# Cluster assignment by pair, later maxima, bulk digits and a new plan in a fused attention and mixture-of-experts kernel

## The chip, the cores and the metric

The kernel runs on one core of one Trainium2 chip, as one launch. The metric is the device time of one execution in microseconds. Five engines work side by side: TensorE (PE in the profile, its weight loads PEld), VectorE (DVE), ScalarE (ACT), GpSimd (POOL) and SyncE (SP), which here issues nearly all transfers. Each engine takes its instructions in the order in which the program lists them for it, and waits in front of the first one that is not ready.

## The reference

Inputs: q, k and v of 4 batches, 8 heads, 768 positions and width 64; 16 centroids a head; a gate matrix 512x8; for 8 experts w1 (512x1024) and w2 (1024x512).

```
q_assign = argmax(normalised q . normalised centroid), k_assign likewise
scores   = q k^T / 8, replaced by -1e9 where q_assign != k_assign
x        = softmax(scores) v, written as 3072 tokens x 512
expert   = argmax(x @ w_gate), gate = its softmax weight
each expert keeps its 80 tokens of largest gate
out[token] = gate * (relu(x[token] @ w1[e]) @ w2[e]), 0 for all other tokens
```

## The kernel before, in words

**Attention.** The 32 heads go in 16 pairs, four to a batch. Both heads of a pair lie in one 128-partition tile of k (`ldk`) and of q (`ldq`). For each head an operand KAB and an operand QAB are put together in SBUF: the high and the low part of the values (a cast on ScalarE, a subtraction on GpSimd, `pair`, L245), and 16 rows with the one-hot code of the cluster, all of it copied into place by small transfers on SP's queue (`copy`, L71). A query whose cluster has no key is masked there.

The cluster codes come from `assign` (L188): a matmul with the normalised centroids, a transpose, a maximum and an equality on VectorE, a transpose back, a matmul that settles ties, and an evacuation on ScalarE. It runs once a batch for k and once for q, over all four pairs, in two halves of 384 columns.

A pair is 12 units, a unit being one head and one chunk of 128 keys. In a unit, TensorE computes scores twice. `sm` (L432) has queries on the partitions, and VectorE takes each row's maximum from it (`mx`, L434). Six such maxima of a head are gathered in `mr`, transposed on TensorE (L452), evacuated on ScalarE (`row`, L455), and a 3 KB transfer on SP's queue writes them as one more row into QAB. After that `st` (L469, then L470, which holds this row) has keys on the partitions, ScalarE takes the exponential (`pp`, L475), GpSimd adds the six chunks of a head (`sum`, L484), and TensorE multiplies with the values (`av`, L493). So the first `st` of a head cannot start before its row has landed. Finished heads are transposed, scaled, and written out as tokens `xs`, with logits and gates for each batch.

**Maxima for scaling.** While attention runs, the 32 blocks of w1 are loaded once, one after the other, into a single buffer (`weigh`, L1333), and VectorE takes each one's largest magnitude (`most`, L1335). `most` is also taken from every pair's values (`ldv`, L1324). These maxima set the scales of the half-precision operands of the experts. Each of these reductions stands in VectorE's one queue, among the `mx`.

**Selection and experts.** `digits` (L627) cuts every gate's bits into five digits and compares them with all digit values; `select` (L684) finds each expert's 80th largest gate digit by digit, a count on TensorE for each digit. Then tokens are gathered and the experts run: `hp` (L1013) and `yp` (L1041). The second matrix of an expert is either split in a high and a low part (three matmuls of two halves each, 48 instructions) or taken as plain fp32 (named in `native2`; 16 instructions that run longer).

**What sets the order.** The kernel builds its instruction lists itself. Work is cut into steps (an engine, an assumed cost, what it needs, a due time `at`) in lanes; `Flow.run` picks, step by step, the engine that could start first, and on it the step that is due first. So the numbers in `CFG`, the assumed costs and the due times set the order on every engine, and nothing is decided at run time. Where TensorE would stand idle by the plan, `fill` (L1511) puts in small matmuls whose results are not used (L1418, here called fillers).

## Time and profile before

| | us |
|---|---|
| three runs | 641.37, 635.55, 641.95; median 641.37 |
| the profiled execution | 639.99 |
| its span, first to last instruction | 638.0 |
| TensorE busy in the span | 590.8 |
| VectorE | 430.8 |
| GpSimd | 405.2 |
| ScalarE | 333.0 |

The profile is of one execution, whose span is 2 us shorter than its own time. Matmuls are pipelined, so groups of matmuls overlap, and a group's mean is longer than the distance from one to the next. The clock column is the mean granted clock of TensorE as a part of 2.4 GHz; 0.50 is 1.2 GHz. A stretch's length less its busy time on TensorE times the clock is the time that TensorE lost in it, by waiting or by the lower clock.

### The profile page before, as it was taken

Reading aid. Unit: us, or ns where it says so; the run is one execution under the profiler, and the core shown is the slowest. Engines: PE = TensorE matmul, PEld = TensorE weight load, DVE = VectorE, ACT = ScalarE, POOL = GpSimd, SP = SyncE. Lnnn points to the kernel's source line nnn. Section 1 sums busy time; section 2 is a strip of 40 time slices with the busy share of each in tenths; the row PEclk is TensorE's granted clock in tenths of the full one; section 3 lists DMA queues with packets and bytes.
Section 4 is the critical chain, followed back from the end, with each engine's and each line's share of the span. In section 5 each row is a group of like instructions: output and inputs, shape, how many; then the busy total and the mean of one; then the engine's idle time right before and its main releaser. Section 6 shows DMA issues by size and latency. Waiting matters only on the chain.

```text
span 638.0 us, 12227 instructions
## 1 busy us (share of the span) xinstructions
PE 590.8 (93%) x4516; PEld 402.2 (63%) x4516; DVE 430.8 (68%) x798; ACT 333.0 (52%) x706; POOL 405.2 (64%) x231
## 2 busy tenths in 40 slices
PE   8979999899969899997799988999999798999996
PEld 6666566566646666655466665666666488777664
DVE  4945677676557665764577766777779467789983
ACT  6543456565535556553355754565556270358850
POOL 5355486879567658966566778598698420454472
PEclk9998999999979899998799998999999979999999
DMA  8477755779967456999485489747593184699911
GB/s 274 100 222 169 196 160 155 173 200 280 221 191 184 142 156 157 237 314 198 125 206 142 114 216 232 207 106 190 155 340 129 28 338 160 240 363 325 397 36 32
DMA packets 71995, 124.55 MB, mean 195 GB/s; under 512 B 10848, under 2 KB 36096, under 8 KB 71936
## 3 DMA queue, kind: packets, MB, share of 16 engines
q1 hardware_dynamic: 70912, 121.12, 66.6%
q0 software_dynamic: 1024, 2.64, 1.3%
q8 instruction: 36, 0.59, 0.4%
q14 instruction: 23, 0.19, 0.1%
HBM read 70.97 MB, written 13.99 MB: 133 GB/s over the span
## 4 chain that ended last, share of the span: by engine, by line
PE 59%; DMA 19%; issue 10%; DVE 5%; SPq 3%; ACT 2%; POOL 2%; POOLq 0%; ACTq 0%; DVEq 0%
PE av L493 18%; PE sm L432 11%; PE st L469 10%; PE st L470 9%; DMA out_dram<-room,si 7%; DMA weigh<-in_w_dram 4%; SPq L72 3%; DMA xg<-xs,gi 2%; DMA QAB<-ohq 2%; PE misc L531 2%; PE misc L203 2%; PE misc L514 1%; DVE mx L434 1%; POOL xg L952 1%; DMA ldv<-in_v_dram 1%
## 5 line engine op out<-in xcount | busy, mean ns | idle before, releaser
L434 DVE TENSOR_REDUCE mx<-sm 128x1 f32<-128x384 f32 x384 | 202.5, 552 | 99.3 <-PE sm L432 96.7
L484 POOL TENSOR_TENSOR sum<-sum,pp 128x768 f32<-128x768 f32 x128 | 231.9, 1833 | 56.9 <-ACT pp L475 56.4
L475 ACT ACTIVATE pp<-st 128x384 f32<-128x384 f32 x384 | 177.5, 493 | 131.4 <-PE st L470 118.3
L432 PE MATMUL sm<-KAB,QAB 80*128 80x384 f32 x384 | 139.2, 387 | 21.7 <-DVE mx L434 8.5
L493 PE MATMUL av<-pp,ldv 128*64 128x384 f32 x768 | 142.9, 505 | 0.0
L469 PE MATMUL st<-QAB,KAB 128*128 128x384 f32 x384 | 138.9, 362 | 0.1
L470 PE MATMUL st<-QAB,KAB 81*128 81x384 f32 x384 | 134.9, 351 | 1.3 <-DMA QAB<-row 1.3
L432 PEld LDWEIGHTS sm<-KAB,QAB 80*128 80x128 f32 x384 | 72.1, 197 | 64.2 <-issue 22.9
L484 POOL TENSOR_TENSOR sum<-pp 128x768 f32<-128x768 f32 x32 | 58.6, 1847 | 59.7 <-ACT pp L475 54.4
L493 PEld LDWEIGHTS av<-pp,ldv 128*64 128x64 f32 x768 | 49.9, 139 | 62.1 <-issue 58.8
L469 PEld LDWEIGHTS st<-QAB,KAB 128*128 128x128 f32 x384 | 76.3, 199 | 7.4 <-issue 5.2
L470 PEld LDWEIGHTS st<-QAB,KAB 81*128 81x128 f32 x384 | 76.6, 199 | 1.6 <-DMA QAB<-row 1.6
L1335 DVE TENSOR_REDUCE most<-weigh 128x1 f32<-128x1024 f32 x32 | 38.9, 1215 | 29.1 <-DMA weigh<-in_w_dram 29.1
L1418 PEld LDWEIGHTS <-one 128*128 128x128 f16 x742 | 44.6, 101 | 5.6 <-issue 2.8
L952 POOL DMA_INDIRECT xg<-xs,gi x8 | 20.0, 2503 | 43.9 <-issue 26.8
L1071 POOL DMA_INDIRECT out_dram<-room,si x8 | 26.0, 3254 | 29.1 <-DVE room L1066 20.5
L298 POOL TENSOR_TENSOR ldq<-ldq,hi 128x768 fp32r<-128x768 f32 x15 | 27.4, 1829 | 16.5 <-ACT hi L292 16.4
L268 POOL TENSOR_TENSOR ldk<-ldk,hi 128x768 fp32r<-128x768 f32 x15 | 27.3, 1822 | 6.4 <-DVE mx L434 6.4
L1013 PEld LDWEIGHTS <-w1p 128*128 128x128 f16 x768 | 28.4, 100 | 3.1 <-issue 3.1
L1418 PE MATMUL tot<-K,one 128*128 128x128 f16 x447 | 29.8, 227 | 0.0
L1013 PE MATMUL hp<-xt,w1p 128*128 128x80 f16 x768 | 28.8, 202 | 0.0
L929 DVE SCALAR_TENSOR_TENSOR w1p<-raw,scales,w1p 128x1024 f16<-128x1024 f32 x22 | 27.8, 1275 | 0.0
(246 smaller groups left out, 663.2 us busy)
## 6 DMA issues: line engine op xcount, KB each, us to landing
raw<-in_w_dram SPq DMA_DIRECT2D x38, 512.0 KB
weigh<-in_w_dram SPq DMA_DIRECT2D x32, 512.0 KB
KAB<-hi SPq DMA_DIRECT2D x60, 192.0 KB
QAB<-hi SPq DMA_DIRECT2D x30, 384.0 KB
room<-in_w_dram SPq DMA_DIRECT2D x22, 512.0 KB
ldk<-in_kT_dram SPq DMA_DIRECT2D x16, 384.0 KB
ldq<-in_qT_dram SPq DMA_DIRECT2D x16, 384.0 KB
ldv<-in_v_dram SPq DMA_DIRECT2D x16, 384.0 KB
```

The source lines that it names most:

```text
L298: nc.gpsimd.tensor_tensor(lo, t, hi.bitcast(F32), op=ALU.subtract)
L432: nc.tensor.matmul(s, lhsT=qj, rhs=k[0:D + C, 0, f * HS:(f + 1) * HS], start=True, stop=True)
L434: nc.vector.tensor_reduce(mx[:, j, f:f + 1], s, axis=AX.X, op=ALU.max)
L469: nc.tensor.matmul(s, lhsT=k[:, 1, ks], rhs=q[:, 1, qs], start=True, stop=False)
L470: nc.tensor.matmul(s, lhsT=k[0:D + C + 1, 0, ks], rhs=q[0:D + C + 1, 0, qs], start=False, stop=True)
L475: self.nc.scalar.activation(self.st["pp", g, c][:, f], self.st.pop(("s", g, c, f)), AF.Exp, scale=float(self.D) ** -0.5)
L484: eng.tensor_tensor(flat(t), flat(a), flat(self.st["pp", g, c]), op=ALU.add)
L493: nc.tensor.matmul(a[i * D:(i + 1) * D, f, 0:HS], lhsT=v[:, c, i, :], rhs=st["pp", 2 * r + i, c][:, f], start=(c == 0), stop=(c == NC - 1) ...
L929: nc.vector.scalar_tensor_tensor(t[:, 1], raw, s, t[:, 0], op0=ALU.mult, op1=ALU.subtract)
L1013: nc.tensor.matmul(hp[:, f, :], lhsT=wt[:, a, fs], rhs=xt[:, x, k, :], start=(k == 0 and i == 0), stop=(k == K - 1 and i == 2))
L1335: nc.vector.tensor_reduce(self.most[:, R + n:R + n + 1], t, axis=AX.X, op=ALU.max, apply_absolute_value=True)
L1418: nc.tensor.matmul(out, lhsT=self.one16, rhs=self.K16[:, 0:n], start=True, stop=True, skip_group_check=True)
```

## The change

- Assignment: `assign` takes one pair, with the two halves of k and the two of q in the four quarters of the partitions. It is listed with the start of pair r for pair r+2, before `pair`. Codes are copied in 16x384 pieces, 8 transfers a pair in place of 4. One matmul with one column and two small VectorE operations are added to each chain.
- Loads: k and q have three buffers each in place of five. The load of pair r+3 waits for pair r's last use of its buffers; before, all eight loads of a batch were listed at the start of the batch ahead of it. `pps` gives nine exponential buffers in place of seven.
- Maxima: the due time of a `weigh` maximum moves from unit u+3 to u+6 and its load is taken to end 6 later than it was; a `ldv` maximum moves by four units and waits for an `av` of the pair before. The weigh loads start at unit 8 and are 4.5 units apart (16 and 5.1 before).
- The last six additions of exponentials run on VectorE (before all 160 on GpSimd).
- `digits` computes all five digits in six operations a call. It is called twice: for the first 18 columns and for the last batch's 6.
- Six experts, not four, take w2 as plain fp32.
- A filler's assumed cost is one value. There are 272 fillers in all, 742 before: 53, 69 and 150 in the tiles misc, st and tot, 190, 105 and 447 before.
- All due times and several assumed costs have new values.

The diff, cut to its core:

```diff
-CFG = dict(at=dict(sum=-3.18, av=5.0, xT=4.47, lt=0.61, turn=5.75, sm=3.25, exp=-0.88, mx=-0.86), stick=1.93, wait=0.03,
-           idle=0.25, dummy=128, bias=1.2, side=(9.63, 3.62, 26.8, 0.78), prep=(-0.91, 0.1), lead=(-39.88, -34.2, -42.52, -44.97,
-           -19.27), zero=(-15.03, 0.1, -6.09, -0.08, -10.39, 0.67), start=dict(pe=6.1, act=4.8, dve=7.5, pool=2.5, dma=0.0),
-           warm=48, nab=6, pps=7, sums=8, xts=4, vs=2, skew=4, raws=4, weigh=(16, 5.1), slots=(15, 9), native1=(), native2=(0, 2,
-           4, 6), early=((2, 6), 185.8), scaled=(), spread=(), mix=dict(ld=-24.41, st=-20.84, hi1=-8.36, lo1=-10.24, hi2=-13.6,
-           lo2=3.85, xg=-31.7, xp=-16.32, out=11.04, sc=-11.17, a0=4, a1=2, a2=3, spare=0.15))
+CFG = dict(at=dict(sum=0.05, av=6.35, xT=17.0, lt=4.45, turn=9.29, sm=1.01, exp=-3.24, mx=-0.7), stick=1.88, wait=0.06, idle=0.25,
+           dummy=128, bias=0.52, side=(-1.86, 0.07), prep=(0.22, 0.32), lead=(-39.03, -34.88, -36.45, -49.02, -17.95),
+           zero=(-12.17, 0.04, -13.76, 0.26), start=dict(pe=6.1, act=4.8, dve=7.5, pool=2.5, dma=0.0), warm=48, nab=6, pps=9,
+           sums=8, xts=4, vs=2, skew=4, raws=4, lds=3, keys=1, adds=6, weigh=(8, 4.5, 6.0), slots=(16, 8), native1=(), native2=(0,
+           1, 2, 3, 4, 5), early=((2, 6), 185.8), scaled=(), spread=(), mix=dict(ld=-27.65, st=-20.84, hi1=-8.36, lo1=-6.37,
+           hi2=-5.09, lo2=3.68, xg=-34.07, xp=-7.98, out=8.16, sc=-9.03, a0=6, a1=2, a2=5, spare=0.15))
-            t = self.ld.tile([P, self.S], F32, name="ld" + n, bufs=self.NP + 1)
+            t = self.ld.tile([P, self.S], F32, name="ld" + n, bufs=CFG["lds"])
-    def assign(self, b, n):
-
-        nc, S, C, NC, NP, HS, w, st = self.nc, self.S, self.C, self.NC, self.NP, self.HS, self.work, self.st
-        G = 2 * NP
-        R = G * C
-        NJ = HS // P
-
-        aside = b == 0 and n == "q"
-        lock = "spare" if aside else "misc"
 ...
+    def assign(self, b, p):
+
+        nc, C, HS, w, st = self.nc, self.C, self.HS, self.work, self.st
+        k, q = st["k", b, p], st["q", b, p]
+        NJ, G = HS // P, P // C
+        r = b * self.NP + p
+        fs = [slice(f * HS, (f + 1) * HS) for f in range(2)]
+        yield Step("pe", .71, needs=["cdiag", ("ld", "k", b, p), ("ld", "q", b, p)], take="misc", key=("sim", b, p), kind=2, seq=True)
+        sim = self.misc([P, HS])
+        for i, (t, f) in enumerate(((k, 0), (k, 1), (q, 0), (q, 1))):
+            nc.tensor.matmul(sim[32 * i:32 * i + 32, :], lhsT=self.cdiag[:, p, :], rhs=t[:, fs[f]],
+                             start=True, stop=True, tile_position=(0, 32 * i))
+        yield Step("act", .5, give="misc")
 ...
+        yield Step("act", .58, also=("dve", .75), needs=[("hi", "q", *divmod(r - 2, self.NP))] if r > 2 else [])
+        oh = st["oh", b, p] = w.tile([P, HS], F32R, name="oh", bufs=2)
+        nc.scalar.activation(oh[0:64], fi[0:64, 0:HS], AF.Identity, bias=self.negone[0:64])
+        z = w.tile([P, 1], F32, name="z", bufs=2)
+        z16 = w.tile([P, 1], F16, name="zh", bufs=2)
+        nc.vector.tensor_reduce(z[0:64], fi[0:64, 0:HS], axis=AX.X, op=ALU.max)
+        nc.vector.tensor_scalar(z16[0:64], z[0:64], 0.5, None, op0=ALU.is_gt)
+        yield Step("pe", .1)
+        nc.tensor.matmul(fi[:, HS:HS + 1], lhsT=self.twos[0:64], rhs=z16[0:64], start=True, stop=True)
+        yield Step("dve", .15)
+        ne = w.tile([P, 1], F32, name="ne", bufs=2)
+        nc.vector.tensor_scalar(ne, fi[:, HS:HS + 1], 0.5, BIG, op0=ALU.is_gt, op1=ALU.mult)
+        yield Step("act", .58, give="misc", key=("oh", b, p))
+        nc.scalar.activation(oh[64:P], fi[64:P, 0:HS], AF.Relu, scale=ne[64:P])
-                r = (2 * p + i) * C
-                copy(AB[g][D:D + C, 0, :], self.st["oh" + n, b][r:r + C, :])
-            if p == self.NP - 1:
-                flow.end["onehot", n, b] = flow.end["hi", n, b, p]
+                for f in range(2):
+                    r = 64 * (n == "q") + 32 * f + i * C
+                    copy(AB[g][D:D + C, 0, f * HS:(f + 1) * HS], self.st["oh", b, p][r:r + C, :])
-        yield Step("none", 0.0, needs=[("oh", "k", b)], key=("hi", "k", b, p), dma=[.14] * 2)
+        yield Step("none", 0.0, needs=[("oh", b, p)], key=("hi", "k", b, p), dma=[.1] * 4)
-            nc.tensor.matmul(mask, lhsT=self.sel[:, p, :], rhs=self.st["ohq", b][:, fs], start=True, stop=True)
-            yield Step("dve", .5, give="misc")
 ...
-        for l, (sh, d0, ge, pre) in enumerate(self.levels):
-            nk = ge.shape[2]
-            di, pi = T("di"), T("pi")
-            key = [("ge", l), ("pre", l)] if t0 else [None, None]
-            yield Step("dve", .5 if t0 else .95, key=key[0], port=BOTH)
-            nc.vector.tensor_scalar(di, bits, sh, 31 if l else 63, op0=ALU.logical_shift_right, op1=ALU.bitwise_and)
-            at = self.view["iota"][:, d0 + 1:d0 + nk + 1]
-            nc.vector.tensor_tensor(ge[:, t0:t1], di.unsqueeze(2).broadcast_to([P, n, nk]),
-                                    at.unsqueeze(1).broadcast_to([P, n, nk]), op=ALU.is_ge)
-            if sh:
-                yield Step("dve", .36 if t0 else .5, key=key[1], port=BOTH)
-                nc.vector.tensor_scalar(pi, bits, sh, (1 << (26 - sh)) - 1, op0=ALU.logical_shift_right, op1=ALU.bitwise_and)
-                nc.vector.tensor_tensor(pre[:, t0:t1], self.OH[:, t0:t1], pi.unsqueeze(2).broadcast_to([P, n, E]), op=ALU.mult)
+        yield Step("dve", 1.2 if long else .8, key=None if long else ("ge", 0), port=BOTH)
+        nc.vector.tensor_scalar(m, self.G[:, js].bitcast(I32), (1 << 26) - 1, None, op0=ALU.bitwise_and)
+        nc.vector.tensor_tensor(pi, m.unsqueeze(1).broadcast_to([P, L, n]), self.sh.unsqueeze(2).broadcast_to([P, L, n]), op=ALU.logical_shift_right)
+        nc.vector.tensor_tensor(self.ge0[:, js], pi[:, 0].unsqueeze(2).broadcast_to([P, n, n0]), iota(self.lowest, n0).unsqueeze(1).broadcast_to([P, n, n0]), op=ALU.is_ge)
+        yield Step("dve", .95 if long else .4, key=None if long else ("pre", 0), port=BOTH)
+        nc.vector.tensor_tensor(self.part[:, :, js], self.OH[:, js].unsqueeze(1).broadcast_to([P, L - 1, n, E]),
+                                pi[:, 0:L - 1].unsqueeze(3).broadcast_to([P, L - 1, n, E]), op=ALU.mult)
+        yield Step("dve", 2.6 if long else 1.1, key=None if long else ("ge", 1), port=BOTH)
+        nc.vector.tensor_scalar(di, pi[:, 1:], 31, None, op0=ALU.bitwise_and)
+        nc.vector.tensor_tensor(self.ge[:, :, js], di.unsqueeze(3).broadcast_to([P, L - 1, n, 31]),
-        for p in range(NP):
+        for p in range(CFG["lds"]):
-            if b + 1 < B and (p, k) == (0, 0):
-                flow.add(*(Lane(loads(b + 1, n)) for n in "kq"))
-                A = CFG["side"]
-                later(side, (self.assign(b + 1, "k"), A[0], A[3]), (self.assign(b + 1, "q"), A[1], A[3]))
             if k == 0 and r + 2 < R:
                 b2, p2 = divmod(r + 2, NP)
+                later(side, (self.assign(b2, p2), *CFG["side"]))
-                yield Step("dve", .88, key=("span", r), needs=[("ldv", r)], at=NU * r - 2)
+                yield Step("dve", .88, key=("span", r), needs=[("ldv", r)] + [("av", r - 1, 3 // K * K + K - 1)] * (r > 0), at=NU * r + 2)
-                yield Step("dma", 1.46, key=("wl", n), needs=[("st", units[u][0] * NC + units[u][1], 0)] + [("wm", n - 1)] * (n > 0), at=u)
+                yield Step("dma", 1.46, key=("wl", n), late=CFG["weigh"][2], needs=[("st", units[u][0] * NC + units[u][1], 0)] + [("wm", n - 1)] * (n > 0), at=u)
-                yield Step("dve", 1.15, key=("wm", n), needs=[("wl", n)], at=u + 3)
+                yield Step("dve", 1.15, key=("wm", n), needs=[("wl", n)], at=u + 6)
-                yield Step("pool", 1.82, alt=("dve", .92) if t >= N - 3 else None, port=BOTH, key=("sum", g, c), needs=[("exp", t, 1), ("exp", when[g, 0], 1)] + room, at=t + at["sum"])
+                yield Step(*(("dve", .95) if t >= N - CFG["adds"] else ("pool", 1.82)), port=BOTH, key=("sum", g, c), needs=[("exp", t, 1), ("exp", when[g, 0], 1)] + room, at=t + at["sum"])
-            d = CFG["dummy"] / 2350 * (1 if self.work.get(tick - 1, 0.0) >= 3060 else 2)
+            d = CFG["dummy"] / 1175
```

How it moves instructions, at three places.

TensorE between the transpose of a second head's maxima (L452, now L448) and the first `st` that needs the row. First the kernel before, fifth pair; the row goes into QAB_101, whose first `st` stands three rows below the last one shown:

```order
L452 MATMUL misc<-K,mr 6x128
L493 MATMUL av<-pp,ldv 64x384 x8
L432 MATMUL sm<-KAB_108,QAB_102 128x384 x2
L469 MATMUL st<-QAB_99,KAB_105 128x384
L470 MATMUL st<-QAB_99,KAB_105 128x384
L469 MATMUL st<-QAB_99,KAB_105 128x384
L470 MATMUL st<-QAB_99,KAB_105 128x384
L469 MATMUL st<-QAB_100,KAB_106 128x384
L470 MATMUL st<-QAB_100,KAB_106 128x384
L493 MATMUL av<-pp,ldv 64x384 x4
L432 MATMUL sm<-KAB_108,QAB_102 128x384 x2
L469 MATMUL st<-QAB_100,KAB_106 128x384
```

Then the change, fourth pair; the row goes into QAB_105, and the last row shown is the first that reads it:

```order
L448 MATMUL misc<-K,mr 6x128
L210 MATMUL misc<-K,ss 128x128 x3
L428 MATMUL sm<-KAB_112,QAB_106 128x384 x2
L465 MATMUL st<-QAB_104,KAB_110 128x384
L466 MATMUL st<-QAB_104,KAB_110 128x384
L489 MATMUL av<-pp,ldv 64x384 x4
L510 MATMUL misc<-K,xT 128x128 x3
L428 MATMUL sm<-KAB_112,QAB_106 128x384 x2
L465 MATMUL st<-QAB_105,KAB_111 128x384
L466 MATMUL st<-QAB_105,KAB_111 128x384
```

Before, two sets of `av` and four `sm` with seven `st` stood in between; now one set of four `av`, four `sm`, two `st` and six small transposes.

VectorE around the eighth `weigh` maximum. Of the `mx` in the kernel before, the last five ahead of the maximum are listed after its load, which is issued on SP:

```order
L444 TENSOR_REDUCE mr<-mx 128x6
L434 TENSOR_REDUCE mx<-sm 128x1 x4
L561 TENSOR_SCALAR den<-misc 128x24
L562 RECIPROCAL rec<-den 128x24
L565 TENSOR_TENSOR l<-misc,rec 128x3x8x8
L434 TENSOR_REDUCE mx<-sm 128x1 x2
L561 TENSOR_SCALAR den<-misc 128x24
L562 RECIPROCAL rec<-den 128x24
L565 TENSOR_TENSOR l<-misc,rec 128x3x8x8
L434 TENSOR_REDUCE mx<-sm 128x1
L1335 TENSOR_REDUCE most<-weigh 128x1
```

In the change, nine are:

```order
L1322 TENSOR_REDUCE most<-weigh 128x1
L430 TENSOR_REDUCE mx<-sm 128x1 x3
L232 TENSOR_REDUCE z<-misc 64x1
L233 TENSOR_SCALAR zh<-z 64x1
L430 TENSOR_REDUCE mx<-sm 128x1 x2
L238 TENSOR_SCALAR ne<-misc 128x1
L430 TENSOR_REDUCE mx<-sm 128x1 x3
L440 TENSOR_REDUCE mr<-mx 128x6
L284 SCALAR_TENSOR_TENSOR ldq<-misc,ldq 128x384
L430 TENSOR_REDUCE mx<-sm 128x1 x2
L1322 TENSOR_REDUCE most<-weigh 128x1
```

Over all 32 maxima there were between 1 and 8 such `mx`, median 5; now there are between 6 and 13, median 9, for all but the last two, which have none but other work.

VectorE at the end of attention, before (`most` is followed by the step that makes the scales, and by digits of the first 18 columns):

```order
L1324 TENSOR_REDUCE most<-ldv 128x1
L434 TENSOR_REDUCE mx<-sm 128x1 x7
L444 TENSOR_REDUCE mr<-mx 128x6
L1335 TENSOR_REDUCE most<-weigh 128x1
L1339 TENSOR_REDUCE m<-most 128x1
L1340 TENSOR_REDUCE m<-most 128x8
L650 TENSOR_SCALAR di<-G 128x18
L652 TENSOR_TENSOR dug<-di,K 128x450
L656 TENSOR_SCALAR pi<-G 128x18
L657 TENSOR_TENSOR dug<-OH,pi 128x144
L1345 COPY m<-misc 128x9
L1347 TENSOR_SCALAR mt<-m 128x9
```

and in the change:

```order
L1311 TENSOR_REDUCE most<-ldv 128x1
L644 TENSOR_TENSOR dug<-OH,pi 128x4x144
L647 TENSOR_SCALAR di<-pi 128x4x18
L648 TENSOR_TENSOR dug<-di,K 128x4x558
L1322 TENSOR_REDUCE most<-weigh 128x1
L480 TENSOR_TENSOR sum<-sum,pp 128x768 x6
L1322 TENSOR_REDUCE most<-weigh 128x1
L1326 TENSOR_REDUCE m<-most 128x1
L1327 TENSOR_REDUCE m<-most 128x8
L1332 COPY m<-misc 128x9
L1334 TENSOR_SCALAR mt<-m 128x9
L1335 TENSOR_SCALAR mt<-mt 128x9
```

The bulk digits of the first 18 columns stand ahead of the six additions, and the last maximum and the scales behind them.

## Rows read from the trace of the kernel before

**Rows 1.** The page's first lines: span, and busy time of each engine.

```profile
span 638.0 us, 12227 instructions
...
PE 590.8 (93%) x4516; PEld 402.2 (63%) x4516; DVE 430.8 (68%) x798; ACT 333.0 (52%) x706; POOL 405.2 (64%) x231
```

**Rows 2.** Stretches by stage: from and to, length, busy time of PE, PEld, DVE, ACT and POOL with the number of instructions, granted clock, DMA share, GB/s. They are the attention, its last sums and logits, the selection and gathers, the experts.

```profile
45.00:498.00 453.00, 424.19 (x2384) 277.87 (x2386) 300.98 (x565) 240.53 (x563) 331.17 (x185) 0.95 0.71 188
498.00:511.00 13.00, 9.03 (x112) 4.92 (x108) 4.33 (x13) 2.51 (x6) 4.03 (x2) 0.98 0.14 34
511.00:548.00 37.00, 33.62 (x542) 31.72 (x542) 24.63 (x77) 12.75 (x16) 6.53 (x11) 0.91 0.68 247
548.00:633.00 85.00, 83.83 (x1057) 57.01 (x1057) 69.95 (x76) 50.28 (x66) 42.33 (x13) 1.00 0.69 245
```

**Rows 3.** The same columns for shorter stretches of the attention.

```profile
40.00:55.00 15.00, 11.03 (x88) 8.97 (x87) 3.25 (x6) 4.17 (x10) 10.33 (x7) 0.77 1.00 247
72.00:82.00 10.00, 8.40 (x38) 6.28 (x37) 5.39 (x12) 5.53 (x14) 3.00 (x2) 0.83 0.75 204
120.00:130.00 10.00, 7.78 (x35) 4.28 (x34) 4.00 (x8) 2.97 (x7) 5.94 (x4) 0.83 0.87 220
174.00:190.00 16.00, 10.81 (x54) 6.86 (x53) 9.10 (x22) 4.98 (x12) 11.50 (x7) 0.79 0.67 193
212.00:225.00 13.00, 11.21 (x51) 8.13 (x53) 6.83 (x13) 6.44 (x15) 9.20 (x6) 0.74 0.40 121
...
286.00:300.00 14.00, 10.66 (x68) 7.41 (x65) 6.19 (x14) 4.46 (x10) 8.85 (x6) 0.88 1.04 207
300.00:316.00 16.00, 12.75 (x61) 8.62 (x59) 8.37 (x21) 6.88 (x18) 9.70 (x6) 0.79 0.51 137
...
390.00:400.00 10.00, 8.19 (x37) 4.51 (x36) 4.68 (x10) 2.93 (x7) 6.23 (x4) 0.83 0.84 206
```

**Rows 4.** The same columns for a late stretch of the attention.

```profile
450.00:495.00 45.00, 44.94 (x251) 28.88 (x249) 36.68 (x53) 25.43 (x62) 36.02 (x21) 1.00 0.59 201
```

**Rows 5.** Who waited for whom: us in total, times, longest.

```profile
DVE most L1335 <- DMA weigh<-in_w_dram: 29.1, 16, 5.5
...
DVE most L1324 <- DMA ldv<-in_v_dram: 11.9, 6, 6.5
```

**Rows 6.** The chain of waits, in order of time: start, length, what. Two loads whose maximum stood in the chain.

```profile
174.10 6.61 DMA weigh<-in_w_dram
...
286.12 6.98 DMA ldv<-in_v_dram
```

**Rows 7.** The chain of waits around the row of the fourth head: its transpose, the transfer of the row, and the `st` that reads it.

```profile
71.16 0.11 PE misc L452
...
73.33 3.27 DMA QAB<-row
...
76.65 0.44 PE st L470
```

**Rows 8.** SP's queue in order of time, just ahead of that transfer.

```profile
70.38 2.87 SPq L72 DMA_DIRECT2D KAB<-hi  x4
```

**Rows 9.** TensorE in order of time at the start of the attention: fillers, and the first `sm` behind them.

```profile
40.76 3.12 PE L1418 MATMUL misc<-K,one 128*128 128x128 f16 x53
...
47.84 0.98 PE L432 MATMUL sm<-KAB,QAB 80*128 80x384 f32 x2 [3.97 <-DMA QAB<-ldq]
```

**Rows 10.** TensorE in order of time around the selection: fillers of the first and the second digit, and the count that follows the first.

```profile
513.75 4.23 PE L1418 MATMUL tot<-K,one 128*128 128x128 f16 x42
517.91 0.76 PE L703 MATMUL q<-dug,alive 128*8 128x31 f16 x24
...
520.84 1.40 PE L1418 MATMUL tot<-K,one 128*128 128x128 f16 x22
```

**Rows 11.** VectorE in order of time: a digit of the first 18 columns while GpSimd adds, and a digit of the last batch.

```profile
488.58 2.30 DVE L652 TENSOR_TENSOR dug<-di,K 128x558 f16<-128x558 int32 x1
...
514.19 1.69 DVE L650 TENSOR_SCALAR di<-G 128x6 int32<-128x6 int32 x1
515.91 0.35 DVE L652 TENSOR_TENSOR dug<-di,K 128x186 f16<-128x186 int32 x1
```

**Rows 12.** GpSimd in order of time: its last two additions.

```profile
497.94 4.09 POOL L484 TENSOR_TENSOR sum<-sum,pp 128x768 f32<-128x768 f32 x2
```

**Rows 13.** Groups by line: busy us, mean ns of one, idle time before them.

```profile
L434 DVE TENSOR_REDUCE mx<-sm 128x1 f32<-128x384 f32 x384 | 202.5, 552 | 99.3 <-PE sm L432 96.7
...
L1335 DVE TENSOR_REDUCE most<-weigh 128x1 f32<-128x1024 f32 x32 | 38.9, 1215 | 29.1 <-DMA weigh<-in_w_dram 29.1
...
L945 DVE TENSOR_TENSOR w2p<-raw,w2p 128x1024 fp32r<-128x1024 f32 x8 | 9.4, 1214 | 0.0
```

**Rows 14.** TensorE in order of time in the experts: fillers, one expert's output from plain fp32, and the first and the last `yp` of one with split weights.

```profile
553.78 7.07 PE L1041 MATMUL yp<-room,hh 128*80 128x512 f32 x16
560.98 1.17 PE L1418 MATMUL tot<-K,one 128*128 128x128 f16 x18
...
565.96 0.45 PE L1041 MATMUL yp<-w2p,hh 128*80 128x512 f32 x1
...
571.31 0.39 PE L1041 MATMUL yp<-w2p,hh 128*80 128x512 f32 x1
...
609.96 1.11 PE L1418 MATMUL tot<-K,one 128*128 128x128 f16 x17
```

More of the change, by code (lines that the diff above doesn't have):

```diff
@@ L1428, in stream @@
             flow.add(lane)
[L1429 removed]
+        for lane, g, o, d in zip((side, prep), (self.assign(0, 1), self.pair(0, 1)), Z[::2], Z[1::2]):
             lane.add(g, at=(o, d))
[L1431 to L1433 removed]
+        flow.add(side, prep, last, tail, *(Lane(g()) for g in (scores, exps, adds, spans, weighs, values, ends, maxima, tops, shifts, vs)), *(Lane(loads(n)) for n in "kq"))
         flow.run()
```

163 lines of the change are left out of this document (70 added, 93 removed).

## The prediction

> **What bounds the kernel now.** I read the page first, then the stretches, then the waits and the chain, and last the timelines of the places found. TensorE is busy for 590.8 of 638.0 us, VectorE for 430.8 [rows 1]: TensorE is the bound, and what can be won is where it stands or runs slow. The stretches say where [rows 2]: the attention from 45 to 498 us holds 424.19 us of TensorE at a clock of 0.95, so it lost 453 - 424.19 x 0.95 = 50 us; the experts at the end lose about 1 us of 85. In a good stretch the attention loses nothing: 251 matmul records in 45.0 us at full clock [rows 4], 0.18 us a record. So the 50 us are local, and the shorter stretches [rows 3] show them by the same sum: 6.5 us at 40 to 55, 3.0 at 72 to 82, 3.5 at 120 to 130, 7.5 at 174 to 190, 4.7 at 212 to 225, 4.6 at 286 to 300, 5.9 at 300 to 316, 3.2 at 390 to 400. The rest is scattered.
>
> The four of 174 to 316, 22.7 us together, have one cause. VectorE waited 29.1 us for blocks of w1 and 11.9 us for values [rows 5]. A load that stood in the chain took 6.6 to 7.0 us [rows 6], and the maximum that needs it stands in VectorE's one queue ahead of the `mx`; TensorE's `sm` waits for `mx`, and when it stands its clock falls too (0.74 to 0.88 there [rows 3]).
>
> **The change part by part**, in us against the profiled execution of 640.0 (2 over its span); the median of the runs is 641.4, and 1% of that, 6.4 us, is about what a measurement of this kernel can tell from no change.
>
> *Maxima placed later, B: -20.* Per maximum 5 `mx` stood between a load and its use, now 9. At 0.552 us each [rows 13] that is 2.8 us of VectorE's work against 5.0, and since an `mx` comes at TensorE's pace (10 or so a 5-unit block, one in about 1.2 us: 453 us for 384), it is about 6 us of time against 11. A load needs up to 7.0 [rows 6]: before it was just short, now it is met with 4 us to spare. What hides it is the queue of `mx`; where it is gone, at the end, two maxima stand behind the additions and cost 1.2 us each [rows 13]. Ends: -22.7 (all four stretches clean) and -8 (loads that queue behind more transfers take 11 us or more). I take -20, near the clean end, since 4 us of slack is more than half a load.
>
> *Start, A: -6.* At 40.76 TensorE ran fillers for 3.12 us and then waited 3.97 us for the last copy into QAB [rows 9]; the stretch lost 6.5 us beside the fillers [rows 3]. The change takes two half chains of assignment and two loads from in front of this, yet its pair 1 transfers still stand around the first row on SP's queue, and eleven more `sm` (2.0 us at 0.18) stand ahead of the first `st`. Ends -9.6 and +2; I take two thirds of the gain.
>
> *Second heads' rows, D: +9.* This is a cost. The row of a pair's second head was transposed with 12 `av`, 4 `sm` and 7 `st` ahead of the `st` that reads it; an `av` of the program is two records, so 35 records, 6.3 us. Now, for about half the pairs, 4 `av`, 4 `sm` and 3 `st` and six short transposes, 15 records and 6 of about 0.1: 3.3 us. The trace shows what a row needs: transposed at 71.16, its transfer issued at 73.33, landed 3.27 us later, read at 76.65 [rows 7], 5.5 us in all. Of these 2.1 went by behind four other transfers on SP's queue [rows 8]; without them 0.4 + 3.27, some 3.7 to 4.2. Missing per head: 0.4 to 0.9, 15 times 0.6 = 9. Ends: 0, and 15 x 3.0 = 45, the loss of 72 to 82 [rows 3] at every pair. I take 9, since in the new order few transfers stand directly ahead of the rows. The Trainium skill, "DMA: Bandwidth & Descriptors", section on the anatomy of one DMA, gives each transfer a fixed part of about 2.0 us, whatever its size. By that an estimate of the path is 2.4 us, the rows would be hidden and this term nothing; the trace, with 3.27 us for 3 KB, speaks against it.
>
> *More small pieces in the assignment, E: +2.* Fifteen one-column matmuls and 30 small VectorE operations, under 0.3 us each, beside other work; 60 more transfers on SP's queue, where four took 2.87 us to issue [rows 8], so 43 us of SP in 450 us. It delays what stands behind on that queue, rows and copies. Ends 0 and +8 (a late row of 0.6 us in every second pair, and as much for copies).
>
> *Last additions on VectorE, F: -2.* GpSimd's last two ended at 502.03 [rows 12] and the sums on TensorE waited for them. A two-operand VectorE pass over 1024 columns takes 1.214 us [rows 13], so 768 about 0.91, half of GpSimd's 2.05; six are 5.5 us, begun as the exponentials come. Behind them stand a maximum of 1.2 us [rows 13] and the small steps of the scales, ahead of the logits' evacuations on VectorE. Ends -4 and +1.
>
> *Selection, G: -6.* After the first digit, 42 fillers run from 513.75 to 517.98 while the digit they cover was done at 516.26 [rows 10, 11]: 1.7 us too many. Later digits have 22 fillers of 1.40 us behind a step, against 0.35 us of VectorE with its predecessor [rows 10, 11], 0.4 too many each. Bulk digits also take some 0.9 us of VectorE out of each of the last levels, and the first level no longer has the 1.69 us operation that stood while GpSimd worked [rows 11]: 1.7 + 3 x 0.4 + 3 x 0.9 is 5.6. The 18-column operations ran 2.30 us [rows 11] under GpSimd's additions; they now stand ahead of the additions, off TensorE's path. Ends -9 and 0.
>
> *Experts, H: +0.5.* A plain output took 7.07 us, a split one 571.70 - 565.96 = 5.74 [rows 14]; two more plain ones cost 2.7, as TensorE is the bound there (83.83 of 85.00 [rows 2]). Fillers cost 0.065 us each there (1.17 us for 18, 1.11 for 17 [rows 14]); four blocks with 65 of them, 4.3 us, become 18 in all, about 1.1: -3.2. With fewer fillers the clock can start lower; at 1.2 GHz for the first few matmuls 0 to +4, I take 1. The casts spared on ScalarE and VectorE lie beside TensorE's work.
>
> *Other stalls of the attention, C: 0.* The 9.7 us at 72, 120 and 390 and the scattered rest come from the same work in another order. Ends -8 and +5. The third loads' buffers and nine exponential buffers: nothing, a load has a pair's time, some 28 us, against 7.
>
> Sum: -20 - 6 + 9 + 2 - 2 - 6 + 0.5 = -22.5, so **618 us**.
>
> **The rivals.**
> 1. *Rows late everywhere, slower than before.* The one mechanism: the `st` of the second head waits behind SP's queue as at 72 to 82, 3.0 us at 15 pairs: +45 in place of +9, 654 us. It decides from (22.5 + 9 + 6.4) / 15 = 2.5 us a row. For it: the distance is 3.3 us and the one row that was that close did stall. Against: at that place four copies stood ahead of it [rows 8]. Chance 0.08.
> 2. *The stalls change place.* Sixty more transfers make loads later, maxima again stand in `mx`'s way: B -8, A -3, G -2, C and the others as they are: 638 us. For it: the DMA share was 0.71 over the attention [rows 2] and 1.00 or more where it stalled [rows 3]; against: there were whole batches of loads at once there, now single ones. Chance 0.20. That the change does not do what it says I exclude for the order (it is in the lists), not for the time.
> 3. *Everything is met.* Rows land in time (D 0), and a third of C goes (-5): 604 us. For it: most stretches of attention lose nothing [rows 4]. Chance 0.19.
> 4. *The clock.* Where TensorE stood its clock was 0.74 to 0.88 of full [rows 3], and in the selection, where fillers ran nearly all the time, 0.91 [rows 2]. Without 297 of the 447 fillers in tot the counts of five digits (0.76 us each at the first [rows 10]) and the start of the experts run at 1.2 GHz: G about -1, H +4, 626 us. The Trainium skill, "TensorE: Matmul & The Clock Gate", part 1, says the low clock is the default and activity lifts it; by that this rival is the rule, the rows above agree, and only how much of the work there is on the path is open. Chance 0.13.
>
> My forecast itself has 0.40. The predicted time is 618; the range 600 to 643 takes in rivals 2, 3 and 4 and leaves out the first and the far ends. Faster by over 1%: 0.40 + 0.19 + 0.13 and a quarter of rival 2, 0.77; within 1%: the rest of rival 2, 0.15; slower: 0.08.
>
> **What would show it.** B: the wait of `most` for `weigh` and `ldv`, 41 us now, under 8, and no stretch of the attention below 0.9 of clock around such a maximum. D: `st` L466 in the chain or in the waits with "QAB<-row", about 0.6 us each time; if they are absent, rival 3. A: less than 4 us lost from 35 to 55 us. G: from the last logits to the last digit 6 us less, with few fillers; a clock of 0.5 there is rival 4. H: experts about as long as 85 us. I am wrong if attention still loses 40 us, or if VectorE's wait for loads stays over 25 us.

## The result, and the profile after

The change takes 614.45 us (median of 4 runs, 612.2 to 615.43) against 638.96 us before (635.55 to 641.95): a ratio of 0.961, with a 95% interval of 0.955 to 0.968. In a later comparison it was 617.4 against 636.57 us, 0.973 (0.969 to 0.978). So a difference of 3 us between kernels of different comparisons says nothing here, and the runs of one kernel in one comparison are 3 to 16 us apart.

The prediction was 618 (600 to 643), and the profiled span moved by -25.0 where -22.5 was forecast. The total came out near, but by luck: errors in the stages cancel, as the table below shows. The page after, for [rows 1]:

```profile
span 613.0 us, 11364 instructions
...
PE 569.8 (93%) x4030; PEld 372.6 (61%) x4030; DVE 421.0 (69%) x824; ACT 317.8 (52%) x694; POOL 395.3 (64%) x225
```

I divided both traces at the same events on TensorE: the first `av`, the last sums and logits, the first count over the last batch's digits, the last digit's closing matmuls, the first expert's `hp`. Before:

```profile
53.36 1.51 PE L493 MATMUL av<-pp,ldv 128*64 128x384 f32 x8
...
501.46 2.79 PE L531 MATMUL sm<-sum,unit 128*32 128x384 f32 x32
...
511.92 0.31 PE L703 MATMUL q<-dug,OH 128*8 128x25 f16 x6 [2.50 <-DVE dug L652]
...
533.45 0.38 PE L696 MATMUL nb<-K,nf 8*128 8x8 f32 x2
...
550.35 3.60 PE L1013 MATMUL hp<-xt,w1p 128*128 128x80 f16 x96
```

After:

```profile
51.20 1.51 PE L489 MATMUL av<-pp,ldv 128*64 128x384 f32 x8
...
475.55 2.79 PE L527 MATMUL sm<-sum,unit 128*32 128x384 f32 x32
...
486.35 0.31 PE L695 MATMUL q<-dug,OH 128*8 128x25 f16 x6 [2.73 <-DVE dug L642]
...
503.63 0.59 PE L688 MATMUL nb<-K,nf 8*128 8x8 f32 x2 [0.74 <-DVE j L729]
...
522.85 5.24 PE L1005 MATMUL hp<-xt,w1p 128*128 128x80 f16 x96
```

| stretch | before | after | difference | forecast |
|---|---|---|---|---|
| start to the first `av` | 53.4 | 51.2 | -2.2 | A -6 |
| first `av` to the last sums | 448.1 | 424.4 | -23.8 | B, C, D, E, F: -11 |
| sums to the first count | 10.5 | 10.8 | +0.3 | |
| first count to the last digit | 21.5 | 17.3 | -4.3 | G -6 |
| last digit to the first expert | 16.9 | 19.2 | +2.3 | 0 |
| first expert to the end of the span | 87.7 | 90.2 | +2.5 | H +0.5 |

The attention gave twice what I had summed up, and all behind it gave nothing (+0.9) where I had 5.5. The first row is not quite like for like: 36 `sm` stand ahead of the first `av` now, 30 before, so about 1.1 us of work (six at 0.18 us) moved from the second row into the first.

Counted by pairs (48 `st` each), most of the attention's gain sits in the first pairs of the batches 1 to 3, the pairs around whose start most loads for the next batch were issued in a row before: they took 33.3, 35.0 and 38.2 us from their first `st` to the next pair's, and take 25.0, 30.2 and 29.5 now. That is 21.8 of the 27.3 us between the first `st` and the last sums. Three of the four stretches with waits for maxima lie in or next to them as well [rows 3], so this alone does not tell the two causes apart.

The stretches after, for [rows 2, 4] (columns as there): the attention, the selection with the gathers, the experts.

```profile
51.00:475.00 424.00, 407.26 (x2372) 261.59 (x2372) 291.54 (x578) 247.39 (x575) 319.32 (x178) 1.00 0.72 198
...
485.00:527.00 42.00, 31.11 (x380) 27.31 (x381) 27.89 (x73) 10.26 (x14) 12.94 (x12) 0.63 0.64 230
527.00:610.00 83.00, 80.45 (x912) 48.68 (x908) 62.94 (x71) 30.50 (x45) 39.47 (x14) 1.00 0.68 244
```

The attention now loses 424 - 407 = 17 us at a mean clock of 1.00, where it lost 50 [rows 2]. VectorE's waits for loads [rows 5] are gone: the group of the w1 maxima has no idle time ahead of it. What TensorE waits for there is the row of a second head. From the page, and from the waits of who for whom:

```profile
L1322 DVE TENSOR_REDUCE most<-weigh 128x1 f32<-128x1024 f32 x32 | 38.6, 1207 | 0.0
```

```profile
PE st L466 <- DMA QAB<-row: 9.5, 9, 2.0
...
PE misc L235 <- DVE zh L233: 2.6, 7, 0.8
```

The chain shows such a row, for [rows 7]: transposed at 64.42, transferred from 64.94, right behind the issue of one load on SP's queue, read at 68.86. Below it stands the row with the longest wait.

```profile
64.42 0.22 PE misc L448
...
64.94 3.87 DMA QAB<-row
...
68.86 0.44 PE L466 MATMUL st<-QAB,KAB 81*128 81x384 f32 x1 [0.34 <-DMA QAB<-row]
...
288.53 4.10 DMA QAB<-row
...
292.68 0.44 PE L466 MATMUL st<-QAB,KAB 81*128 81x384 f32 x1 [2.01 <-DMA QAB<-row]
```

From the transpose to the read this is 4.4 us, against a distance of 3.3 us by my count. At this row TensorE stood for 0.34 us; the nine waits range from 0.22 to 2.01 us, about 1 us each in the mean. The transfers that ended them took 3.87 to 4.65 us.

### The profile page after: what moved, and what is told of

Its sections match the earlier page's. It is cut to its first block, busy times and chain, and to the rows that moved or that the text cites. A ratio compares the mean times of both kernels' runs of the same rounds, so it can differ in the third digit from the quotient of the medians.

```text
span 613.0 us, 11364 instructions
## 1 busy us (share of the span) xinstructions
PE 569.8 (93%) x4030; PEld 372.6 (61%) x4030; DVE 421.0 (69%) x824; ACT 317.8 (52%) x694; POOL 395.3 (64%) x225
## 4 chain that ended last, share of the span: by engine, by line
PE 65%; DMA 17%; issue 9%; POOL 3%; DVE 3%; ACT 2%; SPq 1%; POOLq 0%; ACTq 0%; DVEq 0%
PE av L489 19%; PE sm L428 11%; PE st L466 11%; PE st L465 10%; DMA out_dram<-room,si 7%; DMA QAB<-row 6%; DMA xg<-xs,gi 3%; PE misc L527 2%; PE misc L510 2%; PE misc L202 2%; POOL xg L944 1%; PE misc L282 1%; POOL sum L480 1%; PE misc L448 1%; ACT row L451 1%
## 5 line engine op out<-in xcount | busy, mean ns | idle before, releaser
L471 ACT ACTIVATE pp<-st 128x384 f32<-128x384 f32 x384 | 174.4, 491 | 103.4 <-PE st L466 94.5
L480 POOL TENSOR_TENSOR sum<-sum,pp 128x768 f32<-128x768 f32 x122 | 220.0, 1833 | 5.3 <-ACT pp L471 4.5
L466 PE MATMUL st<-QAB,KAB 81*128 81x384 f32 x384 | 131.7, 343 | 9.5 <-DMA QAB<-row 9.5
L465 PE MATMUL st<-QAB,KAB 128*128 128x384 f32 x384 | 134.0, 349 | 0.0
L466 PEld LDWEIGHTS st<-QAB,KAB 81*128 81x128 f32 x384 | 73.8, 192 | 12.5 <-DMA QAB<-row 12.5
L465 PEld LDWEIGHTS st<-QAB,KAB 128*128 128x128 f32 x384 | 73.6, 192 | 6.7 <-ACT pp L471 3.2
L944 POOL DMA_INDIRECT xg<-xs,gi x8 | 24.8, 3095 | 34.0 <-issue 18.4
L1063 POOL DMA_INDIRECT out_dram<-room,si x8 | 23.9, 2985 | 33.3 <-DVE room L1058 30.1
L1322 DVE TENSOR_REDUCE most<-weigh 128x1 f32<-128x1024 f32 x32 | 38.6, 1207 | 0.0
L1014 ACT ACTIVATE hh<-hp 128x320 f32<-128x320 f32 (+1 forms) x16 | 7.0, 438 | 43.0 <-PE hp L1005 43.0
L1406 PEld LDWEIGHTS <-one 128*128 128x128 f16 x272 | 20.5, 117 | 8.0 <-issue 5.1
L514 ACT COPY x<-misc 128x384 f32<-128x384 f32 x32 | 15.4, 481 | 17.5 <-PE misc L510 17.5
```

Source lines behind the costliest of these rows:

```text
L465: nc.tensor.matmul(s, lhsT=k[:, 1, ks], rhs=q[:, 1, qs], start=True, stop=False)
L466: nc.tensor.matmul(s, lhsT=k[0:D + C + 1, 0, ks], rhs=q[0:D + C + 1, 0, qs], start=False, stop=True)
L471: self.nc.scalar.activation(self.st["pp", g, c][:, f], self.st.pop(("s", g, c, f)), AF.Exp, scale=float(self.D) ** -0.5)
L480: eng.tensor_tensor(flat(t), flat(a), flat(self.st["pp", g, c]), op=ALU.add)
L944: nc.gpsimd.indirect_dma_start(out=xg[0:Mb], out_offset=None, in_=self.xs[:, :], in_offset=bass.IndirectOffsetOnAxis(ap=gi[0:Mb, e:e + 1], ...
L1322: nc.vector.tensor_reduce(self.most[:, R + n:R + n + 1], t, axis=AX.X, op=ALU.max, apply_absolute_value=True)
```

## The experiments

Theory: the gain is that of the maxima (B), less the late rows (D); small items at the end. Rivals: the quieter loads or the new order as a whole made the gain; the clock or the fillers set the end. Each kernel was compared with the one before on its own chip: fill_more, row_slack, max_at_load and plain_four on one, max_alone, load_burst, digits_single and sums_gpsimd on a second, change_again, row_slack_25, exp_seven and no_fillers on a third. The planner makes the list anew for each, so an edit can move other instructions too; TensorE's order without the fillers is that of the change in no_fillers, up to the experts in digits_single, and up to the last sums in sums_gpsimd. The assignment by pair was not undone by itself: what it is worth, or costs, is open.

### The maxima

In the change, the padding of the load that moves the maxima back is taken out:

```diff
-  weigh=(8, 4.5, 6.0)
+  weigh=(8, 4.5, 0.0)
```

> The change with the assumed landing of a w1 block no longer lengthened by 6 us, so that the planner puts each maximum right behind its load again: 4 reductions of scores stand between them in the median, not 9. If it is the place of the maxima that removed the waits of 41 us, VectorE waits 20 to 30 us for these loads again and the time rises by 12 to 20 us, to about 630. If the loads are simply quicker now, for want of whole batches of loads beside them, it stays within 3 us of 614.

630.74 us (627.7 to 639.36, 10 runs), ratio 0.994 (0.989 to 1.000). VectorE waited again, even longer than before, and the attention lost 439 - 414.71 x 0.97 = 37 us. The last two lines are its first `av` and its last sums:

```profile
DVE most L1322 <- DMA weigh<-in_w_dram: 45.0, 16, 8.7
```

```profile
51.00:490.00 439.00, 414.71 (x2351) 267.42 (x2351) 295.94 (x580) 249.14 (x573) 318.71 (x177) 0.97 0.70 192
...
48.78 1.51 PE L489 MATMUL av<-pp,ldv 128*64 128x384 f32 x8
...
492.32 2.79 PE L527 MATMUL sm<-sum,unit 128*32 128x384 f32 x32
```

So the place of the maxima is worth 13 to 16 us of time in the change (against its two medians, of other comparisons), and 19.2 us between the first `av` and the last sums (443.5 against 424.4); the start and the end of this kernel are shorter. The loads stood one at a time here, so quieter loads alone do not remove the waits. Then that part alone, in the kernel before:

```diff
-  ... key=("span", r), needs=[("ldv", r)], at=NU * r - 2)
+  ... key=("span", r), needs=[("ldv", r)] + [("av", r - 1, 3)] * (r > 0), at=NU * r + 2)
 ...
-  ... key=("wl", n), needs=...
+  ... key=("wl", n), late=6.0, needs=...
 ...
-  ... key=("wm", n), needs=[("wl", n)], at=u + 3)
+  ... key=("wm", n), needs=[("wl", n)], at=u + 6)
```

> The kernel before with only the due times of the maxima and the assumed landing of w1 blocks taken from the change: 9.5 reductions of scores stand in the median between a load and its maximum, 5 before. If the place of the maxima is worth what undoing it in the change cost (16 us), the waits of 41 us for loads go and the time falls to 617 to 623. If the new order brings other waits, above all rows whose distance is short here for four second heads (0.7 to 2.7 us), about 628. If the gain belongs to the change as a whole, 636.

638.05 us (635.8 to 643.61), ratio 1.011 (0.997 to 1.024): no gain. The third case came true. The waits did fall, from 41 to 11 us, and `most` for `ldv` does not wait at all:

```profile
DVE most L1335 <- DMA weigh<-in_w_dram: 11.2, 5, 6.2
```

```profile
48.67 1.51 PE L493 MATMUL av<-pp,ldv 128*64 128x384 f32 x8
...
495.84 2.79 PE L531 MATMUL sm<-sum,unit 128*32 128x384 f32 x32
...
549.01 4.65 PE L1013 MATMUL hp<-xt,w1p 128*128 128x80 f16 x96
```

The last sums came at 495.84, 5.6 us earlier than before, but 4.7 of these were there at the first `av` (48.67 against 53.36). Between the two it took 447.2 us, 448.1 before: 30 us less of waiting for loads, and 0.9 us won (2.0 with the six `sm` that stand ahead of the first `av` before and behind it here). By pairs, the second one took 38.6 us (31.4 before): its chain shows transfers into KAB and QAB of up to 3.84 us, and the clock was 0.51 from 80 to 90 us. From the sums to the first `hp` it then took 53.2 us (48.9 before) and from `hp` to the end of the span 92.7 (87.7). The last four maxima fall behind the last `mx` there, in front of the scales, and the rest of the plan was made for other times. The profiled execution is the slowest of the four, so these sizes are rough. An edit of a due time can be an edit of the whole list: undone in the change it costs 13 to 16 us, done alone in the kernel before it brings none.

### The loads of k and q

> The change with the loads of k and q as before: five buffers each, and all eight loads of the next batch listed at the start of a batch; to make room, seven exponential buffers in place of nine. If these bursts caused the other stalls of the attention (some 14 us of the kernel before, which I had forecast to stay and which went), 6 to 14 us come back: 620 to 628. If not, 614 within 3 us.

```diff
-  ... pps=9, ... lds=3, ...
+  ... pps=7, ... lds=5, ...
 ...
-  for r in range(CFG["lds"], R):
-      yield Step("dma", 1.09, needs=self.taken(n, *divmod(r - CFG["lds"], NP)), ...
+  for r in range(NP, R):
+      yield Step("dma", 1.09, needs=[("burst", r // NP)] + (self.taken(n, *divmod(r - CFG["lds"], NP)) if r >= CFG["lds"] else []), ...
 ...
+  if b + 1 < B and (p, k) == (0, 0):
+      flow.end["burst", b + 1] = flow.now
```

622.79 us (621.41 to 626.06), ratio 0.989 (0.974 to 1.004). Two buffers of exponentials went too, so they were taken alone in a further run, with the one edit `pps=9` to `pps=7`:

> The change with seven exponential buffers in place of nine, loads as in the change: the part of load_burst that is not the bursts. If bursts alone cost the 8.5 us there, this stays within 3 us of change_again; if the two buffers do, it comes to about 622.

610.91 us (609.32 to 617.15), ratio 0.964 (0.957 to 0.971). So the two buffers cost nothing that shows, and the bursts 12 us by the medians (of two chips) and 9 us by the traces, from the first `av` to the last sums (431.3 against 421.9). In the trace a burst shows as a slow row. SP's queue of load_burst, and the chain: six of the eight loads are issued in a row, then four copies, then the row. Last, what `st` waited for rows in all:

```profile
144.02 1.52 SPq L184 DMA_DIRECT2D ldk<-in_kT_dram  x3
145.59 1.78 SPq L184 DMA_DIRECT2D ldq<-in_qT_dram  x3
...
151.25 6.98 DMA QAB<-row
...
PE st L466 <- DMA QAB<-row: 8.3, 4, 3.8
```

Its 3 KB took 6.98 us, against 3.87 above, and one `st` waited 3.8 us for it; in exp_seven four such waits come to 2.5 us. The first pairs of the batches 1 to 3 took 106.9 us together with bursts and 96.0 without (106.5 in the kernel before, 84.7 in the change); all others were 1.4 us shorter with bursts. The attention with bursts, then without (both with seven buffers):

```profile
53.00:483.00 430.00, 411.69 (x2371) 263.43 (x2372) 293.23 (x576) 248.73 (x574) 319.00 (x178) 0.98 0.69 191
```

```profile
51.00:472.00 421.00, 410.42 (x2374) 262.30 (x2374) 291.55 (x586) 247.02 (x575) 319.38 (x178) 0.99 0.72 199
```

### The rows

The planner is told that a row lands 1.5 us later, and in the second kernel 2.5:

```diff
-  key=("shift", g), dma=[.06]
+  key=("shift", g), dma=[.06], late=1.5
-  self.end[step.key] = d
+  self.end[step.key] = d + step.late
```

> The change with the planner told that a row lands 1.5 us later, so that it puts other work ahead of the first st of a second head: by matmul counts the distance grows from mostly 3.3 us to mostly 4.6. If rows issued just before use are what costs the change some 9.5 us, that wait falls below 3 us and the time by 5 to 9, to about 607. If the wait only changes place, or other work comes late in its stead, 614 within 3 us.

> The change with rows planned to land 2.5 us later (1.5 in row_slack): the distance for second heads becomes 5.0 in the median, with two of 2.0 and 2.8 left. If late rows cost the change what its waits show, 9.5 us and the clock behind the longer ones, the waits stay under 4 us and the time is 5 to 9 below change_again, about 607. If what is won goes into other waits, it is within 2 us of change_again.

row_slack: 610.19 us (607.95 to 613.12), ratio 0.960 (0.951 to 0.969). row_slack_25: 614.71 us (608.72 to 617.04), ratio 0.967 (0.962 to 0.973), beside the change itself in the same comparison:

> The change itself once more, beside the three others on one chip, as what they are compared with: 614 within 3 us, and 9 to 10 us of waits of st for rows.

617.4 us (615.42 to 621.5), 0.973 (0.969 to 0.978). The waits went as expected (to 2.9 us), the time by 2.7 us where 5 to 9 were expected, and the two intervals overlap. The waits of row_slack, then its first `av` and last sums:

```profile
PE st L466 <- DMA QAB<-row: 1.3, 2, 0.8
```

```profile
54.30 2.80 PE L489 MATMUL av<-pp,ldv 128*64 128x384 f32 x16
...
475.28 2.79 PE L527 MATMUL sm<-sum,unit 128*32 128x384 f32 x32
```

From `av` to the sums 421.0 us, 3.4 less than in the change; but the first `av` is 3.1 later. In row_slack_25 the first `av` stands at 56.25 and the sums at 475.33: 5.7 us less than change_again (51.34, 476.15) between the two, 4.9 more ahead of them. Part of both differences is work that changed sides. Six more `st` stand ahead of the first `av` in these kernels, and three more `sm` in the one, seven in the other: at 0.18 us each that is 1.6 and 2.3 us. Without it, 1.8 and 3.4 us were won between `av` and the sums, and 1.5 and 2.6 lost ahead of them, since the longer assumed landing also holds back the very first rows, where no other work is at hand. So the late rows cost about 2 to 3 us of the 9.5 that TensorE waits, and what this experiment won it mostly gave back at the start. A later landing for second heads alone was not tried.

### The end: additions, digits, fillers, experts

> The change with the last six additions on GpSimd again. At 1.83 us each in place of 0.96 the last one ends 2 to 5 us later if the additions stand in the chain: 616 to 619. If VectorE's last maximum and scales are what the sums wait for, or the last exponentials, 614 within 1 us.

```diff
-  adds=6
+  adds=0
```

621.22 us, but from 611.38 to 625.25, too far apart for a verdict. The traces are clear on the mechanism. GpSimd's last additions, and the sums on TensorE in that run:

```profile
466.77 14.29 POOL L480 TENSOR_TENSOR sum<-sum,pp 128x768 f32<-128x768 f32 x8
```

```profile
480.43 2.81 PE L527 MATMUL sm<-sum,unit 128*32 128x384 f32 x32
```

and VectorE's last one in the change:

```profile
473.45 0.96 DVE L480 TENSOR_TENSOR sum<-sum,pp 128x768 f32<-128x768 f32 x1 [1.19 <-ACT pp L471]
```

GpSimd ends at 481.06, VectorE at 474.41, just ahead of the end of the last `av`; the sums come 4.9 us earlier in the change. Not all of that is the additions. TensorE's matmuls, without fillers, stand in the same order in both kernels up to these sums, and yet the last `av` already started 3.1 us later here. First sums_gpsimd, then the change:

```profile
475.89 2.80 PE L489 MATMUL av<-pp,ldv 128*64 128x384 f32 x16
```

```profile
472.82 2.80 PE L489 MATMUL av<-pp,ldv 128*64 128x384 f32 x16
```

From there to the sums it took 4.54 and 2.73 us: 1.8 us are seen to belong to the additions. 0.96 us is the estimate of 0.91.

> The change with the digits one by one as before, 18 operations a call in place of 6; attention as it is. If bulk digits are what shortened the five counts by 4.1 us, the time rises by 3 to 5 us, to 618, and it is seen between the first and the last count. If it was the fillers (42 after the first digit before, 20 now), it stays within 1.5 us of 614.

Here `digits` and the keys it is awaited by are those of the kernel before. 617.24 us (614.01 to 624.67), ratio 0.983 (0.962 to 1.003). The first and the last piece of the counts:

```profile
484.87 0.31 PE L699 MATMUL q<-dug,OH 128*8 128x25 f16 x6 [2.50 <-DVE dug L648]
...
501.89 0.59 PE L692 MATMUL nb<-K,nf 8*128 8x8 f32 x2
```

17.0 us against 17.3 with bulk digits: the bulk form brought nothing that shows (the planner put 68 fillers between the two here, 51 in the change). Then the fillers, 598 and none in place of 272:

```diff
-  d = CFG["dummy"] / 1175
+  d = CFG["dummy"] / 2350
```

> The change with every filler assumed to take half as long, so that the planner puts 598 in place of 272 into the same gaps; every other instruction stands where it stood. If the low clock (0.63 from 485 to 527 us) is what kept the selection and the start of the experts from gaining, the clock there rises above 0.85 and the time falls by 3 to 6 us, to about 609. If fillers stand in the way of the counts, as they did after the first digit in the kernel before, it rises by 1 to 4 us. If neither, 614 within 1 us.

```diff
-            self.idle(n, misc)
```

> The change with none of its 272 fillers, all other instructions where they stood. If the clock of the start, the selection and the first expert hangs on them, the clock there goes to 0.50 throughout and the time rises by 3 to 8 us, to 617 to 622. If the path there is VectorE's and the transfers', it stays within 2 us of change_again, as it did with twice as many.

With 598 fillers 616.33 us (613.63 to 617.64), ratio 0.970 (0.961 to 0.978); with none 613.13 us (609.76 to 613.34), 0.964 (0.958 to 0.969). The counts in both:

```profile
488.47 0.31 PE L695 MATMUL q<-dug,OH 128*8 128x25 f16 x6 [2.73 <-DVE dug L642]
...
505.47 0.38 PE L688 MATMUL nb<-K,nf 8*128 8x8 f32 x2
```

```profile
486.10 0.31 PE L695 MATMUL q<-dug,OH 128*8 128x25 f16 x6 [2.73 <-DVE dug L642]
...
501.27 0.59 PE L688 MATMUL nb<-K,nf 8*128 8x8 f32 x2 [1.51 <-DVE j L729]
```

The five counts took 17.0 and 15.2 us, 17.3 in the change. Between these two events the columns of [rows 2] are, for fill_more, no_fillers and the change:

```profile
488.47:505.47 17.00, 17.00 (x254) 15.57 (x253) 9.22 (x38) 7.81 (x11) 3.56 (x8) 0.84 0.73 280
```

```profile
486.10:501.27 15.17, 10.32 (x130) 9.33 (x129) 10.41 (x39) 8.03 (x11) 3.45 (x8) 0.50 0.91 346
```

```profile
486.35:503.63 17.28, 16.46 (x182) 14.11 (x181) 10.41 (x39) 7.83 (x11) 3.27 (x8) 0.50 0.81 304
```

So the counts of the change already ran at 1.2 GHz, and taking its 51 fillers from between them only took work out of the way: 2.1 us. With 124 fillers there, fill_more had a clock of 0.84 and won 0.3 us. The kernel before had 204 and 0.87, and took 21.5 us. The first case of no_fillers failed, and with it my fourth rival; it came out 4.3 us below change_again, more than the 2 us of its second case.

> The change with four experts (0, 2, 4, 6) taken with plain w2 in place of six, as before; attention is the same instruction for instruction, and the planner puts 296 fillers into the tile tot in place of 150. If two more plain outputs cost TensorE 1.33 us each, and nothing else, the experts get 2.7 us shorter and the time about 612. If the casts that they spare ScalarE and VectorE are worth more, it rises to 616 or more.

```diff
-  native2=(0, 1, 2, 3, 4, 5)
+  native2=(0, 2, 4, 6)
```

625.66 us (619.15 to 629.82), ratio 0.982 (0.972 to 0.993). Its profiled execution is the slowest of the four (629.82 us), 6 us longer than the change in the attention, so only its experts are read: 99.5 us from the first `hp` to the end of the span, 9.3 more than in the change, though its outputs on TensorE are shorter. TensorE between its first and second expert, and ScalarE's wait there:

```profile
539.85 5.97 PE L1406 MATMUL tot<-K,one 128*128 128x128 f16 x104
```

```profile
542.68 0.62 ACT L955 CAST room<-xg 80x512 f16<-80x512 f32 x1 [7.03 <-DVE xg L950]
```

The second expert's tokens come late: ScalarE waits 7.03 us for VectorE, and TensorE runs 104 fillers. Four subtractions of a split w2 (L937) stand ahead of this one in VectorE's queue, so in this order the casts and subtractions of a split w2 are on the path at the start of the experts. In the kernel before, with an order of its own, four plain experts did not wait so: its first two `hp` are 11.64 us apart, 18.36 here, 13.21 in the change.

## Why the prediction was right or wrong

- **B, maxima later (-20).** The mechanism was right in the change: 5 reductions were too short for a load of 7 us, 9 are enough, and the 41 us of waits went to none. Undone it costs 19.2 us between the first `av` and the last sums, and 13 to 16 us of time. It does not stand alone, though: in the kernel before the same edit won 1 to 2 us there.
- **C, other stalls of the attention (0), and the loads.** This is the step that failed, "the same work in another order", together with "The third loads' buffers and nine exponential buffers: nothing". Bursts of loads cost 9 to 12 us when they are put back: transfers of rows run into six loads at once. I had named them in rival 2 (DMA share 1.00 where it stalled [rows 3]) and not drawn the sum from it. The three stretches that I had put under C are not among them: no load of k or q was issued at 72 to 82, 120 to 130 or 390 to 400 us (the nearest is a single one at 69.9). TensorE waited there for the row behind four copies, for a transfer of tokens, and for something that the profile does not tell; which edit removed these three was not tested.
- **D, late rows (+9).** TensorE waits 9.5 us for them, as much as forecast in sum, but in 9 places at about 1 us, not in 15 at 0.6. What they cost in time is about 2 to 3, so the term was three times too large or more, by what the two row_slack kernels gained between the first `av` and the sums. The first rival, 3.0 us at each of 15 pairs, did not come. The Trainium skill, "DMA: Bandwidth & Descriptors", section on the anatomy of one DMA, has its fixed part of about 2.0 us under a heading on DMAs that GpSimd issues, while SyncE issues these rows; it would have made this term nothing. Of the traces, those of quiet moments agree (1.84 us at 405.05 in exp_seven), and those at the late rows do not: 3 KB took 3.87 us here, and 6.98 in a burst.
- **E (+2).** The new one-column matmul waits 2.6 us in seven places for VectorE. That is about the size of the term; what it costs in time, and what the 60 more transfers cost, was not tested.
- **A, start (-6).** -2.2, or some -3.3 without the six `sm` that changed sides. The fillers and the wait went, but not all of the loss: from 35 to 55 us TensorE now lost 5.4 us by the low clock, where I had asked for less than 4 (before, 6.5 from 40 to 55 alone [rows 3]):

```profile
35.00:55.00 20.00, 19.49 (x91) 14.16 (x91) 13.06 (x29) 11.12 (x25) 11.87 (x7) 0.75 0.73 191
```

- **F, additions (-2).** About 1.8 us from the last `av` to the sums: sized right.
- **G, selection (-6).** -4.3, and for one of the two reasons only. Fewer fillers after each count did it, 51 for 204; that bulk digits take 0.9 us out of each level was wrong, those operations lay beside the count already (17.0 against 17.3 us).
- **The gathers (0).** +2.3 us that no step of mine held. The first gather on GpSimd took 3.10 us (1.90 before) and landed later; in row_slack and exp_seven it took 1.90 again, and why was not tried.
- **H, experts (+0.5).** +2.5. The first `hp` took 5.24 us, in good part at the low clock (3.60 at the full one): 1.6, where I took 1. Two more plain outputs cost about the 2.7 that I had: one takes 6.90 us on TensorE from its first matmul to the next step, a split one 5.59. The fillers spared give 1.6 us behind the first `hp`, not 3.2: 47 stood there before, 9 do now, and one block of the 65 stood ahead of it. Together that is 2.7, all of the difference. And "the casts spared lie beside TensorE's work" was wrong in this order, as plain_four shows.
- **Rival 4, the clock.** It fell as it said, 0.63 in the selection, and cost nothing that shows there; only the first expert paid.

In all: attention -23.8 against -11, for the loads (C) and the late rows (D); all behind it +0.9 against -5.5, for the gathers, H and part of G. That the total came out at -25.0 for -22.5 is luck.

No kernel here beats the change by more than the comparisons leave open: row_slack, exp_seven and no_fillers were 610 to 613 us, the change 614 and 617. no_fillers comes nearest: its four runs (609.76 to 613.34 us) all lie below the six of the change beside it (615.42 to 621.5), while the intervals (0.958 to 0.969, and 0.969 to 0.978) touch.

## What to carry to other kernels

A stall that a trace puts down to one late transfer can have its cause in what else was on the queues, as the row of 6.98 us in a burst: before calling other stalls "the same as before", see which transfers were under way in them. With instruction lists planned as a whole, undo a part in the new kernel as well as doing it alone in the old one; the two differ here by 13 to 16 us. Price a wait that the new order creates (needed time less given distance, times how often), and expect less than the whole of it in the end: here 2 to 3 of 9.5 us. When two lists are compared between two events, count the work ahead of the first event in both; here up to 2.3 us had only changed sides.
